# Residual rows and V leave PSUM by half rows; the layer-norm statistics and the row score read SBUF; shorter rstd; a new recorded order

## The chip, the cores and the metric

One core of a Trainium2 chip runs the kernel. The metric is the device time of one execution in microseconds (us), as the median of several runs. Comparisons are between kernels that ran in turn on the same chip, and only runs in the fast state are compared: ratios and intervals use these alone, while a median that is quoted is over all runs of its kernel, slow ones too. Engines are named as in the profile: PE is TensorE, DVE is VectorE, ACT is ScalarE, POOL is GpSimd.

## The reference, cut to what matters

The program is one transformer block over 2048 rows of 576 columns. Attention works on four segments of 512 rows with 32 heads of 18 columns and carries a memory from segment to segment. Then one single row, the one with the highest score, goes through an MLP.

```python
def A(x):                        # attention, S=2048, D=576, H=32, Dh=18, 4 segments of 512
    q, k, v = heads(x @ wq), heads(x @ wk), heads(x @ wv)
    phi = lambda t: where(t > 0, t + 1.0, exp(t))          # the feature map
    for s in range(4):
        p   = softmax(qs @ ks.T * Dh**-0.5 + mask)         # the 160 exponentials of the profile
        o   = (1 - g) * (p @ vs) + g * (phi(qs) @ M) / (phi(qs) @ z + 1e-6)
        M, z = M + phi(ks).T @ vs, z + sum(phi(ks))
    return o @ wo
def B(x):                        # MLP (F=4608) for the row with the highest score
    r = x @ w_r;  i = argmax(r)
    x[i] += sigmoid(r[i]) * ((silu(x[i] @ w_gate) * (x[i] @ w_up)) @ w_down)
    return x
x = x + ga * A(layernorm(x) * (1 + ca) + sa)
x = x + gb * B(layernorm(x) * (1 + cb) + sb)
```

## The kernel before

The kernel registers some thousand small operations, each with one or more engines that may do it, and then issues them in a recorded order. `ORDER` holds, for each place, the number of an operation and the engine chosen for it. It also holds dummy matmuls, which keep TensorE from falling idle.

```python
def recorded(self):
    ...
    for x in struct.unpack("<%dH" % (len(raw) // 2), raw):
        o = self.ops[x // 4]
        o.eng, _, o.emit = o.alts[x % 4]          # operation x//4, by its engine choice x%4
        seq.append(o)
```

The layer norms turn mean and variance into `rstd`, and then normalise a tile of 128 rows by 576 columns on whichever engine the order names.

```python
def rstd_op(mv, rst, i0, n, slot, R, W, eps=True):
    nm_ = nmr[:, slot, 0:n]
    def f():
        if eps:
            nc.gpsimd.tensor_tensor(out=mv[:, i0:i0+n, 1], in0=mv[:, i0:i0+n, 1], in1=epsF[:, 0:n], op=ALU.add)
        nc.gpsimd.tensor_tensor(out=rst[:, i0:i0+n], in0=mv[:, i0:i0+n, 1], in1=mhalf[:, 0:n], op=ALU.pow)
        nc.gpsimd.tensor_tensor(out=nm_, in0=mv[:, i0:i0+n, 0], in1=rst[:, i0:i0+n], op=ALU.mult)
        nc.gpsimd.tensor_scalar(nm_, nm_, -1.0, None, op0=ALU.mult)          # nmr = -mean * rstd
    ...
def norm_alts(dst, src, sc_, mn_, bi_, engs=("POOL", "DVE", "ACT")):
    a = {"POOL": ("POOL", 0.83, lambda: nc.gpsimd.tensor_scalar(dst, src, sc_, bi_, op0=ALU.mult, op1=ALU.add)),
         "DVE": ("DVE", 0.43, lambda: nc.vector.tensor_scalar(dst, src, mn_, sc_, op0=ALU.subtract, op1=ALU.mult)),
         "ACT": ("ACT", ac(576, "S", 1), lambda: nc.scalar.activation(dst, src, ACT.Identity, bias=bi_, scale=sc_))}
```

The feature map is built as min(max(t + 1, 1), exp(t)) in two VectorE operations. V and the output projection collect two halves of 288 columns in two PSUM banks, and the pair is copied out by one operation. The statistics and the score of the residual rows read the same two banks.

```python
# feature map, both on VectorE
nc.vector.tensor_scalar(PH, QT[0:r2, m0:m0 + np_, :], 1.0, 1.0, op0=ALU.add, op1=ALU.max)
nc.vector.tensor_tensor(out=PH, in0=PH, in1=EQK[0:r2, ei, 0:np_, :], op=ALU.min)
...
# residual rows of tile i (output projection plus the input, in PSUM)
g2 = P.psum("M", 2)
...
xp = lambda g2=g2: pair(g2)[:, :, 0:288]
op(alts(("ACT", ..., copy(xo, xp())), ("DVE", ..., tensor_copy(xo, xp()))), ...)       # one copy of 576 columns
ln_stats(lambda g2=g2: (bank(g2, 0)[:, 0:288], bank(g2, 1)[:, 0:288]), mv2[:, i, :], ...)
nc.vector.scalar_tensor_tensor(out=JK..., in0=xp(), scalar=mv2[:, i, 0:1], in1=W1B...,  # the score: x from PSUM
                               op0=ALU.subtract, op1=ALU.mult, accum_out=ra[:, i:i + 1])
rstd_op(mv2, rstd2, i, 1, sl, ...)
nc.gpsimd.tensor_tensor(out=rr[:, i:i+1], in0=ra[:, i:i+1], in1=rstd2[:, i:i+1], op=ALU.mult)
# finish_tile: UB = norm(x1), then three elementwise steps ("WB"), each on VectorE or GpSimd
tt(w_, u_, G1b, ALU.mult, ...); tt(w_, w_, C2b, ALU.add, ...); tt(w_, w_, xo, ALU.add, ...)
```

The softmax here doesn't subtract the row's maximum and nothing guards it: scores larger than these inputs give would overflow.

Of the kernel before, what the change touches and what calls it, by code (L numbers as in the profile page):

```python
# [35 lines left out]
    "Kml+7JOBs)bN~PWGyntu)Btz@>;OmrPynm|002w?3;>7$fB~2Qd;#PDU;vx|i~%?Rpa2j6fB<{|hyaiQumQ9Ix&hb$qyQ)Yr~niIpaIAM`~ZXjlmTo2=mFUP"  # L36
    "m;tZ=Q~+E6qyeA?yaB}lSO7!;!U4<yqz0S;cmeDIv;ffogaF(D)d4^NtOl?K<QM1{>=*DCWCDx;v<9dK@d4ohEC9R)AOP3`^Z_IS6au&g<pBf&C<6Ea7y<|a"
    "zy`Pg@Brul^Z+aZ3<A6WzyL4;r~w=T`~k!OoC4eeXaXSu-~#0WYyuDh^a4Zx00KM#(Ev08WB{N8%?6|cpaOsbtN|PVZ~~+P#Rg0Q7y$SJr~)_w$p%mYbONXY"
    "JOV)ikOQm(<Ob0O=mwYr_y(*3lmo~B%mCZ~=mOvX@CJkeR08w{L;_d>?FNVf00SHYTmp;&)CT<q*aqMRAOi#gBm)QoxB{F5FaT@=_zT?z1Ps6f{0sa73<I<R"
    "a08G6zyibryaIFs01OZVcmu=&$OB9RC<Dj>umjBkPy=8BTmw`Cv;zzbd;$akxC2N6U;}6X%mWAvxCgugkN{)@Sp$>;X#;oyoCnYXJOh9Ogaf<>Km&*ai~}?S"  # L40
    "zz0MF#Rtd-5DW+bNCOxH6bu*)APfuvBn;3400fu<Farbx)dQdh90Aw^2n09-BmfWu6a*Lq90a5X3<MAX_yFAl<O5g-s0ZK!Fb4n!@B{b*^aK0@TnFd_DGclb"
    "7zbbnGzT09AOvIwI0xJZJO?NQAP3+FBnRvQ91J7`umaQqKm>3EH~~cj<Oc)?bOh)JECVbAcmyB;2nP%Y6a#1nC<lB47y&Q@Kn#=sJPb?>SOriFL<|53WC1t?"
    "Tm=vZEDSIVGz3%(1PDnCU<7~%2nc8dWCTD3><2sqI1GdbfCw}U3<&rKR1r)E@B&y7cn63FfCLl)j0c1Sga}9lKnJV`L<NWhOa)vKEC+}PNCa#FbO($GO$1N{"
    "U<ix^pagsbYy@BdWD%qUWC(B!s06G8YzJrvZ3rj`ECEmlSPXmzR0Z@0R0LcMkOY_nv<FlNU<{N5)CY77Y!NI7cnq8bWDL*;Py{dtumpSzkO%MtGzhf>SOhc;"
    "P!U`N*bHD1Xc0IK+zj{x&;$?&^aS7x)CBYlJPr5^Yz1%y{0!IxKn-98*arX&NC@Q&`~=_xxCBrEXay7pcm*H`=mc;P<OF;XWCbJvyaaRwX#s!@PzXc^00sO9"
    "I0&!@R0voB2n7TMzyw$bgbmyTTnJPFfD!Bj%m>5-$OOy;bP+@dc@Zc9a0pBY5Cwb%6a^Rs90iCCbO;m(NCzAUh!G40cnCBBs1b|}@CV=)uneRTd<cXQAO)ZZ"
    "krAvBv<zqrxC|%-B?T}6j1jyHqzI4*s0geGm=P@nkPRdVZ~@2-lo6Z}%ndLF&<)51pb<0$m<W^zoCr7tzz94ANCAip)eXo9PzsC;JP2qCa0gThkPKJ~#0U@#"
# [12 lines left out]
    "@eAAwY!7q~IS+sfJP$k)m<vD;MGp`Y6cgAI7!$Y~yc>BB<O_fgC=aX>EDtabSQ2~>hz~3iFcWMLg%4Q^G!rxr%nOYVkPnp)Gz-8R#2XwFm=7QmoDaww%p1@f"  # L60
    ")En3v+#BE<<Qt3=pbw-EBoO!!Boq7+loP!WC=e(UkQ0~_a1eA5I1?-o025pbcn~lUJQG9{KobNLG!Wz#NE0{^2oro0uo4In%o2bTd=P{ah!cPigb+j!%oaTm"
    "Y!gfnuoiR^ND#;pkPws*OcQVuQ4_cpR1=60q!Z{H>>KbK^c(maOckgTSrd2@P!%i`R1h!}R22jfJO&IA{2Krq1RMw)WEC_N5D~l+z!10)oD+}>#1mW)pcZHq"
    "Y!$>1P!PZqm=K^4SQS_hp%e5ATouR=+!Lh>U=ZXJU=?H#I27O$%n;BJ+z`zZtQOD{$P?5P*%Q?e6cOMM7!hC-TodFFtP`*kv=d|#9TXrGj1Z^`=o7RSxDy-^"
    "*bpQXXcG(^5F8X77#tiNARG-8C=o0Xs1_*{L=+ShArb8m5ERH2sSxxN>=W@5_!FEEKoG4E85C#`un<TT@DL;%C>$&tFdQ@-Y!omNJQO4md=)_y{1fyL02ELZ"
    "OcVqZR1^plSQJDHfE6?mbQGx+v=DF<tQ4>mI1z9abQL%pJRCqAL>%Q5>=bwvq!7RsgcV2}OdL=gR2-NTh!u<#wG`+SycT#AJQ4U1{1E6CK@k8E%@xoUL=n^#"
    "ND&wo@f4sG6c>;cloebQoD{?spcSMQ*cD(D+!dr0WE7|s;1$#q>=u|6ycFCN>=kGfxD@CR<rNebfE0Wbz!a<%gcR@<*c9{?_!U?jTpVB=WE^N5Ar&YU{S}B5"
    "92blfAQzAnloT8m;1u{2Bp37){S*-uBo$y57!@cNEfq`=AQqez$Q1Y%#1zaF1Qh@k2o=y26crs6EEhBt=oJhXFc$z83>736WEQX$XcjaVFcmlzC>A^wKou+&"
    "L={LCcouCIa29+PbQXaYgcdj!JQk1^lotFJv=ulP02jFxKo&$6Y#eYLbR2jbd>nurgdB(*j2u80F&0S{m=>HCkQ|g8m>irOpd6$es2r>uupG1;xE#D3z#POJ"
    "L>EXG$Q;ZZ&>Ykp*c{v(;2h)}=p5`E@Er6U_#FHk038G!P#07eh!$EG2ptR^a2N0vycbLt1r~T0JQuwc^cFN02^PQ=To;TMP!?4d#1#w{5Epb8d>4clfEP>_"
    "2p0qwh!>0(kQbB}z!w-7#1{}2$QNN3WEW@`Y!_J;To%k1&=;5&pckYUoENAUuotWsv=_J+*ca3n+!x>%")  # L70
BANKS = (
    "00IF30S5vB0|o{F00#vE2Lb~nB@;IR6D1Q095(?a0RjL33LG3R3LG2?B>@Kq1_~ts69E$eB@-nD0s;XpHzgba0XHQ90|W#I1_lBF1px#T1rq=_1px*I00#vI"
    "2L=TL0wn=AB@;I{0TTfeH#ZXn1q2fTHxoA#0TUA?1qA^CH#ZXjH#a3WB>)5lB>@T?69F7I903Oa2LU%X69)tZ1_1yi10@1C022TQ1_K8L1p)&E2L%H+0RaIn"
    "903zI0US3RHwFU%0XHQ96E`;{B>?~i2LTfSB{wA{0TTfR2Ld+}6D0v9B@-n#0|EmI3KIbU2LS>%03`td03`(h0tEyG1O);F1popC024P80VM$eHvu;U1p_w|"
    "6E`;{0RjROB@;IR69fkb6D1`#903Ie1`{^{69oYQ6B8u_0uwhk69NY%0XHQB12;D}0R$xm0RsUCB?ABk0s;aD1TFvy1P2EL0|Ns900000000000000000000"
# [81 lines left out]
def mmc(n):  # L157
    return max(n / 2400 + 0.0025, 0.025)
# [11 lines left out]
def kernel(  # L170
# [1160 lines left out]
```

## Time and profile before

| | before |
|---|---|
| time, median of the first three runs | 261.76 us (261.16 to 262.21) |
| span of the profiled run, mean granted TensorE clock | 258.5 us, 0.972 |
| first, last of the 160 exponentials start | 25.8, 227.1 us |
| search for the highest score, MLP, down-projection start | 236.5, 242.5, 251.2 us |

The page's first part gives each engine's busy time, share of the span and number of instructions.

```profile
PE 230.6 (89%) x3447; PEld 142.9 (55%) x3466; DVE 212.6 (82%) x477; ACT 196.9 (76%) x236; POOL 171.5 (66%) x283
```

No engine is alone the limit. GpSimd has the lowest share of the four, 66%. The second part of the page cuts the span into 40 slices and gives the busy tenths of GpSimd in each.

```profile
POOL 6804723854939955596966879739679997818720
```

In the groups of instructions, kept apart by shape, the columns are line, engine, operation, output<-input names and shapes, count, then busy us and mean ns of one, then the idle us just before them and what ended it.

```profile
L748 ACT ACTIVATE arena<-PS 128x1024 bf16<-128x1024 f32 x160 | 152.7, 1028 | 16.8 <-PE PS L730 11.5 <-PE PS L739 2.2 <-POOL mv L541 1.8
...
L884 POOL TENSOR_TENSOR arena<-arena 128x576 bf16<-128x576 bf16 x21 | 27.6, 1320 | 6.0 <-DVE arena L883 5.6
...
L548 POOL TENSOR_SCALAR arena<-arena,rstd,nmr 128x576 bf16<-128x576 bf16 x15 | 13.8, 920 | 0.6
...
L937 DVE SCALAR_TENSOR_TENSOR arena<-PS,mv,arena 128x576 bf16<-128x576 f32 x16 | 13.0, 812 | 0.3
```

L748 are the exponentials: ScalarE idles 16.8 us before them, 11.5 of it for the score matmuls of L730. L548 is GpSimd's normalisation, 0.92 us each. L937 is the row score. The source view of two of these lines gives the least, median and greatest duration in ns.

```profile
L548 POOL TENSOR_SCALAR arena<-arena,rstd,nmr x15: 823/827/1833, 7.6 to 224.5; 128x576 bf16<-128x576 bf16 x15
```

```profile
L937 DVE SCALAR_TENSOR_TENSOR arena<-PS,mv,arena x16: 805/810/819, 102.2 to 233.6; 128x576 bf16<-128x576 f32 x16
```

The score never varies by more than 14 ns. The tail is a chain of single steps. The chain of waits lists start us, us, and what; these are three of its pieces.

```profile
235.20 1.41 DVE arena L549
...
246.08 1.51 DVE arena L883
...
247.68 0.46 DVE arena L883
```

L549 is a normalisation and L883 an elementwise step. The same L883 takes 1.51 us and then 0.46. Last, the table of stretches gives, for 252 to 254 us, the busy time of PE, PEld, DVE, ACT and POOL with counts, then the granted clock, the DMA share and GB/s; the timeline gives start and duration of the down-projection.

```profile
252.00:254.00 2.00, 2.00 (x76) 2.00 (x68) 0.01 (x1) 0.00 (x0) 0.00 (x0) 0.50 0.03 8
```

```profile
251.17 3.78 PE L1279 MATMUL PS<-arena 128*1 128x144 bf16 x144 [0.28 <-DVE arena L1243]
```

The down-projection runs at half clock (0.50) and takes 3.78 us.

### The profile page before, as it was taken

The numbers are of one execution on the slowest core, as the hardware profiler recorded it, in microseconds if no ns is written. First come the engines' busy times: TensorE is split into PE (matmuls) and PEld (weight loads), VectorE is DVE, ScalarE is ACT, GpSimd is POOL, SyncE is SP. The second block draws the span as 40 slices with busy tenths as digits, with TensorE's granted clock in tenths as the row PEclk, the third lists the DMA queues.
The fourth block names the chain that finished last, engine by engine and source line by source line (L and its number), as shares of the span: only waits on it lengthen the run. The fifth ranks groups of instructions, "written<-read, shape, count | busy, mean of one in ns | idle before, by whom it ended". The sixth has DMA issues, their size and how long they took to land. (4 is left out here: it accounts for less than half of the span.)

```text
span 258.5 us, 8600 instructions
## 1 busy us (share of the span) xinstructions
PE 230.6 (89%) x3447; PEld 142.9 (55%) x3466; DVE 212.6 (82%) x477; ACT 196.9 (76%) x236; POOL 171.5 (66%) x283
## 2 busy tenths in 40 slices
PE   7699899989999999999989999799878998887974
PEld 3364465445446566656555655466556766655544
DVE  4847977768999999999989879686879999889470
ACT  3452788888988999999889989599979799942030
POOL 6804723854939955596966879739679997818720
PEclk9979999999999999999999999799999999999787
DMA  5959963555746142474325289554788869998650
GB/s 158 324 161 285 319 184 122 163 165 173 199 115 180 55 116 94 129 230 147 118 71 186 79 251 268 187 170 160 217 268 278 263 218 281 229 326 324 207 191 3
DMA packets 34207, 49.20 MB, mean 190 GB/s; under 512 B 4011, under 2 KB 28210, under 8 KB 34166
## 3 DMA queue, kind: packets, MB, share of 16 engines
q1 hardware_dynamic: 34166, 48.64, 60.8%
q8 instruction: 27, 0.44, 0.7%
q14 instruction: 14, 0.11, 0.1%
HBM read 36.75 MB, written 11.87 MB: 188 GB/s over the span
## 5 line engine op out<-in xcount | busy, mean ns | idle before, releaser
L748 ACT ACTIVATE arena<-PS 128x1024 bf16<-128x1024 f32 x160 | 152.7, 1028 | 16.8 <-PE PS L730 11.5
L759 POOL TENSOR_SCALAR_AFFINE_SELECT arena<-arena 128x1024 bf16<-128x1024 bf16 (+1 forms) x65 | 64.9, 1007 | 37.1 <-ACT arena L748 31.7
L618 PE MATMUL PS<-arena 128*128 128x512 bf16 (+1 forms) x176 | 49.9, 385 | 2.7 <-DVE arena L622 1.0
L730 PE MATMUL PS<-arena 18*128 18x128 bf16 (+2 forms) x736 | 35.3, 259 | 4.7 <-DMA arena<-q_d 1.6
L884 POOL TENSOR_TENSOR arena<-arena 128x576 bf16<-128x576 bf16 x21 | 27.6, 1320 | 6.0 <-DVE arena L883 5.6
L730 PEld LDWEIGHTS <-arena 18*128 18x128 bf16 x736 | 16.1, 92 | 24.6 <-issue 21.4
L684 PE MATMUL PS<-arena 128*128 128x288 bf16 x160 | 26.2, 286 | 0.6 <-ACT arena L748 0.3
L774 PE MATMUL PS<-arena 128*32 128x128 bf16 (+2 forms) x736 | 24.3, 264 | 2.4 <-ACT arena L748 1.1
L618 PEld LDWEIGHTS <-arena 128*128 128x128 bf16 (+1 forms) x195 | 17.2, 102 | 16.6 <-issue 5.4
L920 PE MATMUL PS<-arena 128*128 128x288 bf16 x160 | 25.1, 286 | 1.0 <-ACT arena L748 0.6
L622 DVE CAST arena<-PS 128x512 bf16<-128x512 f32 (+1 forms) x29 | 19.3, 679 | 3.8 <-PE PS L618 1.6
L782 DVE CAST arena<-PS 128x512 bf16<-128x512 f32 (+1 forms) x27 | 17.7, 660 | 4.5 <-PE PS L774 4.3
L774 PEld LDWEIGHTS <-arena 128*32 128x32 bf16 x736 | 14.5, 97 | 11.4 <-issue 3.3
L1293 PE MATMUL PS<-arena 128*128 128x256 bf16 x135 | 19.8, 283 | 0.0
L684 PEld LDWEIGHTS <-arena 128*128 128x128 bf16 x160 | 14.1, 98 | 7.3 <-issue 2.0
L920 PEld LDWEIGHTS <-arena 128*128 128x128 bf16 x160 | 14.0, 97 | 7.0 <-issue 2.5
L541 POOL TENSOR_TENSOR mv<-mv,epsF 128x1 f32<-128x1 f32 (+2 forms) x21 | 4.1, 197 | 20.7 <-DVE mv L533 10.7
L883 DVE TENSOR_TENSOR arena<-arena 128x576 bf16<-128x576 bf16 x27 | 17.1, 645 | 0.2
L668 ACT ACTIVATE arena<-arena 128x1024 bf16<-128x1024 bf16 (+1 forms) x18 | 16.5, 927 | 0.0
L674 DVE TENSOR_TENSOR arena<-arena 126x1024 bf16<-126x1024 bf16 (+1 forms) x18 | 14.7, 819 | 0.5 <-ACT arena L668 0.4
L1293 PEld LDWEIGHTS <-arena 128*128 128x128 bf16 x135 | 12.3, 100 | 5.1 <-issue 3.3
L542 POOL TENSOR_TENSOR rstd<-mv,mhalf 128x1 f32<-128x1 f32 (+2 forms) x21 | 13.8, 657 | 1.6
(206 smaller groups left out, 413.0 us busy)
## 6 DMA issues: line engine op xcount, KB each, us to landing
arena<-in_B_w_down_dram SPq DMA_DIRECT2D x9, 576.0 KB
arena<-in_B_w_up_dram SPq DMA_DIRECT2D x8, 576.0 KB
arena<-in_B_w_gate_dram SPq DMA_DIRECT2D x8, 576.0 KB
arena<-in_A_x_dram SPq DMA_DIRECT2D x28, 144.0 KB
arena<-q_d SPq DMA_DIRECT2D x30, 128.0 KB
arena<-k_d SPq DMA_DIRECT2D x30, 128.0 KB
arena<-in_w_mod_dram SPq DMA_DIRECT2D x3, 1152.0 KB
x_d<-arena SPq DMA_DIRECT2D x16, 144.0 KB
```

Of the source, the lines that this page charges most:

```text
L618: nc.tensor.matmul(bank(g, 0)[0:r], lhsT=lhs(k), rhs=h1T[hb][:, k, :], start=(k == 0), stop=(k == KC - 1))
L622: op(alts(("DVE", dv(512, "P"), lambda g=g, dst=dst, r=r: nc.vector.tensor_copy(dst, bank(g, 0)[0:r])), ("ACT", ac(512), lambda g=g, dst=d ...
L684: nc.tensor.matmul(bank(g, hf)[:, 0:288], lhsT=h1T[hb][:, k, 128 * b:128 * b + 128], rhs=WP["v"][:, k, 288 * hf:288 * hf + 288], start=(k ...
L730: nc.tensor.matmul(bank(gs_[x // 2], x % 2)[:, off:off + b - a], lhsT=KS[32 * x:32 * x + DH, c, 128 * j:128 * j + 128], rhs=QS[32 * x:32 * ...
L748: op(one("ACT", 1.035, lambda g=gs_[x], pt=pt: nc.scalar.activation(pt, pair(g), ACT.Exp, scale=SCALE)), R=[("lt", n)], W=[("PT", pp, x)], ...
L759: om = op(alts(("POOL", 0.68 if pat[0][1] == 4 else 1.12, lambda v4=v4, pat=pat: nc.gpsimd.affine_select(out=v4, in_=v4, pattern=pat, comp ...
L774: nc.tensor.matmul(bank(gp, 0)[32 * x:32 * x + 32, o0 + a - qa:o0 + b - qa], lhsT=va[:, j, 4 * c + x, :], rhs=PT[:, pp, x, off:off + b - a ...
L782: ("DVE", dv(w, "P"), lambda gp=gp, ai=ai, gi=gi: nc.vector.tensor_copy(ASB[ai][:, gi, 0:w], bank(gp, 0)[:, 0:w]))),
L883: op(alts(("DVE", dv(576, acc=2), lambda: nc.vector.tensor_tensor(out=out_, in0=a_, in1=b_, op=o_)), ("POOL", 1.3, lambda: nc.gpsimd.tenso ...
L884: ("POOL", 1.3, lambda: nc.gpsimd.tensor_tensor(out=out_, in0=a_, in1=b_, op=o_))), R=R, W=W, lock=True)
L920: nc.tensor.matmul(bank(g2, hf)[:, 0:288], lhsT=ot[:, k, :], rhs=wop[:, k, 288 * hf:288 * hf + 288], start=(k == 0), stop=False)
L1293: op(one("PE", mmc(256), lambda gF=gF, src_=src_: nc.tensor.matmul(bank(gF, 0)[:, 0:256], lhsT=src_[:, 0:128], rhs=src_[:, 0:256], start=T ...
```

## The change

The intent: free PSUM banks earlier (halves, and statistics and score that no longer hold the banks), move work from VectorE to the less busy GpSimd, drop two of the four small operations of each `rstd`, compute the input statistics of segments 2 and 3 in the head, and record a new order for all of it. The diff, cut to its core:

```diff
@@ ORDER, BANKS: new strings, cut @@
@@ rstd_op, norm_alts @@
-        nm_ = nmr[:, slot, 0:n]
             nc.gpsimd.tensor_tensor(out=rst[:, i0:i0 + n], in0=mv[:, i0:i0 + n, 1], in1=mhalf[:, 0:n], op=ALU.pow)
-            nc.gpsimd.tensor_tensor(out=nm_, in0=mv[:, i0:i0 + n, 0], in1=rst[:, i0:i0 + n], op=ALU.mult)
-            nc.gpsimd.tensor_scalar(nm_, nm_, -1.0, None, op0=ALU.mult)
-    def norm_alts(dst, src, sc_, mn_, bi_, engs=("POOL", "DVE", "ACT")):
-        a = {"POOL": ("POOL", 0.83, lambda: nc.gpsimd.tensor_scalar(dst, src, sc_, bi_, op0=ALU.mult, op1=ALU.add)),
+    def norm_alts(dst, src, sc_, mn_, bi_, engs=("POOL", "DVE")):
+        a = {"POOL": ("POOL", 0.83, lambda: nc.gpsimd.tensor_scalar(dst, src, mn_, sc_, op0=ALU.subtract, op1=ALU.mult)),
@@ head: statistics of segments 2 and 3 (cut) @@
+    def ahead():
+        for s in (2, 3):
+            dma(xa, x_in[L * s:L * s + L, :]..., kb=590)
+            ... ln_stats(...); rstd_op(mv1, rstd1, TPS * s, 4, 0, ...)
@@ feature map @@
-                op(one("DVE", ..., nc.vector.tensor_scalar(PH, QT[...], 1.0, 1.0, op0=ALU.add, op1=ALU.max)), ...)
+                ts_ = lambda e, ...: ENG[e].tensor_scalar(PH, QT[...], 1.0, 1.0, op0=ALU.add, op1=ALU.max)
+                op(alts(("DVE", dv(512 * np_, acc=4), ... ts_("DVE")), ("POOL", 0.13 + 0.62 * np_, ... ts_("POOL"))), ...)
@@ V: the same for the residual rows @@
-            g = P.psum("M", 2)
+            for hf in range(2):
+                g = P.psum("M", 1)
                 ... five matmuls of 288 columns, then one copy of 288 columns
@@ residual rows @@
-            ln_stats(lambda g2=g2: (bank(g2, 0)[:, 0:288], bank(g2, 1)[:, 0:288]), mv2[:, i, :], RP, ..., ps=[g2])
-            op(one("DVE", 0.95, ... scalar_tensor_tensor(out=JK..., in0=xp(), ...)), ..., ps=[g2])
+            ln_stats(lambda xo=xo: (xo[:, 0:288], xo[:, 288:576]), mv2[:, i, :], RX, ...)
+            op(one("DVE", 0.82, ... scalar_tensor_tensor(out=JK, in0=xo, ...)), ...)
-            op(one("POOL", 0.15, ... rr[:, i] = ra[:, i] * rstd2[:, i]))            # for each tile
+            r0 = {7: 0, NT - 3: 8, NT - 2: NT - 2, NT - 1: NT - 1}.get(i)           # four times in all
```

Decoding the two orders shows what the new one does with the choices.

| | before | after |
|---|---|---|
| dummy matmuls | 135 | 106 |
| add/max of the feature map on GpSimd | 0 | 12 |
| elementwise steps at the end of a tile, GpSimd/VectorE | 21/27 | 30/18 |
| normalisations on GpSimd | 15 | 20 |
| copies of V, of residual rows | 16, 16 | 32 halves (25 on VectorE), 32 halves (22 on VectorE) |

## The prediction

> **What bounds the kernel now.** The engine summary shows TensorE busy 89%, VectorE 82%, ScalarE 76%, GpSimd 66%. No engine is alone the limit. In the table of stretches, 60–160 us has ScalarE 93%, VectorE 94% and TensorE 94% busy at full clock, but TensorE there includes idle-filling dummy matmuls (135 of 256 columns, 19.8 us of records). ScalarE's 160 exponentials (1.03 us each) set the floor; they idle 16.8 us in total, 11.5 of it waiting for score matmuls (groups view), which wait for PSUM banks and for VectorE's turn. The last 27 us are a serial tail (chain of waits from 234.4 us on): evacuation 0.67, a normalisation that took 1.41 beside a GpSimd operation (its own fastest: 0.33), top-1, the MLP, three elementwise steps (1.5+0.5 us) ahead of the gate, and a down-projection at granted clock 0.5–0.66.
>
> **What the change does.** I decoded both recorded orders.
> - Dummies fall from 135 to 106; sixteen of these are new in the MLP tail. Before the last tile's scores about 45 go: at 0.11–0.15 us, 5–6 us of TensorE holes closed, less 3 more masked score steps (about 0.5 us).
> - Two-bank residual groups, held through statistics, score product and copy (about 2.5 us after the last matmul at 230.7–235), become single banks freed by a half copy.
> - VectorE: 12 feature max operations (−6 us), 9 elementwise (−5.8) and 2 normalisations go to GpSimd; 6 h1T evacuations arrive (+3.2); copies in halves cost about 0.46 (from 0.55 for 384 and 0.73 for 576 columns), +4 us. Net about −8. ScalarE −3.
> - GpSimd: about −13 us (two operations of each rstd, 12 of 16 score products), but about +30 of moved work: net about +15.
> - Eight statistics (8.8 us VectorE) and 1.2 MB of loads move into the head, where VectorE is 60–85% busy but the DMA share is 1.03 at 20–30 us: I expect the first exponential 0–2 us later (25.8 before).
> - Tail: last copy and normalisation leave VectorE's path ahead of top-1 (−1 to −1.5 us), elementwise work moves ahead of the MLP's end (−0.5 to −1), dummies keep the clock up for the down-projection (−0.5 to −1.2; the Trainium skill, "TensorE: Matmul & The Clock Gate", What's actually happening: half rate after an idle window of about 3.4 us; the trace agrees, 0.50 at 252–254).
>
> **Brakes.** The score product now has two SBUF inputs. The Trainium skill, "SBUF — State Buffer", Who interferes with whom, says such a VectorE instruction and a GpSimd one that reads SBUF exclude each other. The trace agrees for other operations: the elementwise step takes 0.44 to 1.52 us, the normalisation 0.33 to 2.09. With 15 us more GpSimd work and 16 such products I expect these waits to eat about half of VectorE's −8. Estimate: body −2.5, head +0.5, tail −2.5 us.
>
> **Prediction: 257.2 us, 80% range 253.3 to 260.6.** Faster by over 2%: 0.39; within 2%: 0.58; slower: 0.03.
>
> **What would show each step right or wrong.** Dummies about 106. Residual and V copies about 0.46 us on VectorE and 0.42 on ScalarE. ScalarE's waits for score matmuls below 11.5 us. VectorE busy 203–212, GpSimd 182–190 us. Score product mean from 0.81 to 0.8–1.2 us, with a long maximum. Last exponential 2–3 us earlier than 228.1; from there to the end about 2.5 us less. Down-projection clock above 0.8.
>
> **What would make it wrong.** If exclusion between GpSimd and VectorE is mild, the closed holes count in full: 253–255. If the statistics in the head, queued ahead of the first score operands on VectorE, delay the first exponential by over 3 us, or masks now later behind GpSimd's new work stall the probability products, the time stays at 260–262.

## The result, and the profile after

The kernel after takes 294.04 us (median of four runs, 293.72 to 299.05, the last of them slow), beside 261.46 us for the kernel before (median of four). The ratio is 1.1248, with a 95% interval of 1.119 to 1.1306. Ratios here and below are from the fast runs of both kernels in the same rounds, so not quite the ratio of the medians quoted. The result is correct. The mean granted clock of the profiled runs fell too, from 0.972 to 0.924; what that costs by itself was not separated.

The page's first part and GpSimd's row of the second, after:

```profile
PE 237.7 (81%) x3501; PEld 142.2 (49%) x3501; DVE 218.5 (75%) x482; ACT 195.0 (67%) x240; POOL 236.9 (81%) x249
...
POOL 7453594999799999988899249999969999299971
```

GpSimd went from 171.5 to 236.9 us busy, 65 us more, with 34 fewer instructions. I had predicted 182 to 190. Its row is now nearly all 9. The fourth part of the page, the chain that ended last, by engine:

```profile
POOL 36%; PE 32%; DVE 15%; issue 9%; ACT 6%; DMA 1%; SPq 0%; POOLq 0%; ACTq 0%; DVEq 0%
```

GpSimd leads it with 36%. The groups that answer to those of before, with the two of the moved add/max (L685):

```profile
L763 ACT ACTIVATE arena<-PS 128x1024 bf16<-128x1024 f32 x160 | 152.5, 1031 | 36.6 <-PE PS L745 25.2 <-PE PS L754 10.1 <-PE PS L789 0.4
L547 POOL TENSOR_SCALAR arena<-arena,mv,rstd 128x576 bf16<-128x576 bf16 x20 | 49.1, 2458 | 0.8
...
L899 POOL TENSOR_TENSOR arena<-arena 128x576 bf16<-128x576 bf16 x30 | 39.1, 1309 | 3.1 <-DVE arena L898 2.2
...
L685 POOL TENSOR_SCALAR arena<-arena 126x1024 bf16<-126x1024 bf16 x7 | 25.4, 3634 | 0.0
...
L961 DVE SCALAR_TENSOR_TENSOR arena<-arena,mv 128x576 bf16<-128x576 bf16 x16 | 15.4, 960 | 0.1
...
L685 POOL TENSOR_SCALAR arena<-arena 72x512 bf16<-72x512 bf16 x5 | 10.1, 2024 | 0.0
```

```profile
L547 POOL TENSOR_SCALAR arena<-arena,mv,rstd x20: 2285/2320/3252, 13.1 to 272.7; 128x576 bf16<-128x576 bf16 x20
```

```profile
L961 DVE SCALAR_TENSOR_TENSOR arena<-arena,mv x16: 765/814/1556, 110.9 to 268.6; 128x576 bf16<-128x576 bf16 x16
```

Three things are to be seen. GpSimd's normalisation has the same engine, instruction name and shape as before, but takes 2.46 us instead of 0.92; even its fastest took 2.285, against 0.823. That speaks against waiting beside another engine and for an operation that is slower itself; micro, below, tests it. The twelve add/max cost 35.5 us in all; scaling 0.92 us for 576 columns, I had put them near 1.3 us each, some 15.5. And the exponentials now wait 35.3 us (25.2 + 10.1) for matmuls. The elementwise step of L899 costs 1.31 us as before, so GpSimd has not become slower in general.

The sum works out. Twenty normalisations at (2.46 − 0.92) are 30.8 us, the add/max 20.0 more than assumed, together 51 us. That fits the gap between the 236.9 us and the 182 to 190 predicted (47 to 55).

How a long GpSimd operation reaches the exponentials shows in the timeline between 66 and 78 us: start us, us, engine, line, what, and in brackets the idle time before and its releaser.

```profile
66.77 3.66 POOL L685 TENSOR_SCALAR arena<-arena 126x1024 bf16<-126x1024 bf16 x1
...
70.47 6.10 DVE L687 TENSOR_TENSOR arena<-arena 126x1024 bf16<-126x1024 bf16 x1 [2.50 <-POOL arena L685]
...
76.60 1.06 ACT L682 ACTIVATE arena<-arena 128x1024 bf16<-128x1024 bf16 x1 [6.81 <-DVE arena L687]
...
76.99 1.01 PE L632 MATMUL PS<-arena 128*128 128x512 bf16 x2 [7.02 <-DVE arena L705]
```

VectorE waits 2.50 us for GpSimd's add/max; its minimum, L687, then takes 6.10 us beside five GpSimd operations in a row; ScalarE stands 6.81 us and TensorE 7.02. In ScalarE's own timeline no exponential runs between 69.8 and 78.6 us.

In one place the tail looks as was hoped.

```profile
286.00:288.00 2.00, 2.00 (x105) 1.77 (x106) 1.03 (x4) 0.00 (x0) 0.00 (x0) 1.00 0.21 74
```

```profile
286.56 2.42 PE L1306 MATMUL PS<-arena 128*1 128x144 bf16 x144
```

The clock is 1.00 here and the down-projection takes 2.42 us instead of 3.78. That the new dummies did this is not shown: before_norm, an experiment told below, has the tail of the kernel before with none of them, and ran the same matmuls as fast.

```profile
258.75 2.42 PE L1279 MATMUL PS<-arena 128*1 128x144 bf16 x144 [0.28 <-DVE arena L1243]
```

The milestones, read from the timelines, tell where the time went:

| start us | before | after | both | modelled | modelled_score1 |
|---|---|---|---|---|---|
| first exponential | 25.8 | 27.5 | 26.9 | 25.5 | 26.4 |
| 41st | 87.0 | 99.7 | 89.4 | 89.2 | 91.7 |
| 121st | 182.4 | 206.1 | 180.3 | 182.1 | 180.2 |
| last exponential | 227.1 | 260.8 | 231.7 | 231.6 | 228.2 |
| search for the highest score | 236.5 | 273.2 | 242.5 | 242.2 | 237.8 |
| down-projection | 251.2 | 286.6 | 254.8 | 255.4 | 251.0 |
| end of span | 258.5 | 292.4 | 260.6 | 261.2 | 256.8 |

The last exponential starts 33.7 us later, and the whole span is 33.9 longer. The loss lies in the body; the tail is a wash. (The last three columns are experiments told below.)

### The profile page after: what moved, and what is told of

The parts are those of the page before. It is cut to its first block, busy times and chain, and to the rows that moved or that the text cites. A ratio compares the mean times of both kernels' runs of the same rounds, so it can differ in the third digit from the quotient of the medians.

```text
span 292.4 us, 8676 instructions
## 1 busy us (share of the span) xinstructions
PE 237.7 (81%) x3501; PEld 142.2 (49%) x3501; DVE 218.5 (75%) x482; ACT 195.0 (67%) x240; POOL 236.9 (81%) x249
## 4 chain that ended last, share of the span: by engine, by line
POOL 36%; PE 32%; DVE 15%; issue 9%; ACT 6%; DMA 1%; SPq 0%; POOLq 0%; ACTq 0%; DVEq 0%
POOL arena L547 10%; POOL arena L774 9%; PE PS L632 8%; POOL arena L685 7%; ACT arena L763 5%; POOL arena L899 4%; PE PS L935 4%; PE PS L745 3%; DVE arena L916 3%; POOL rstd L543 3%; PE PS L789 2%; PE PS L1320 2%; PE PS L1228 2%; PE PS L652 2%; PE PS L615 1%
## 5 line engine op out<-in xcount | busy, mean ns | idle before, releaser
L763 ACT ACTIVATE arena<-PS 128x1024 bf16<-128x1024 f32 x160 | 152.5, 1031 | 36.6 <-PE PS L745 25.2
L774 POOL TENSOR_SCALAR_AFFINE_SELECT arena<-arena 128x1024 bf16<-128x1024 bf16 (+1 forms) x62 | 61.7, 1009 | 20.5 <-ACT arena L763 20.3
L632 PE MATMUL PS<-arena 128*128 128x512 bf16 (+1 forms) x195 | 57.0, 402 | 8.9 <-DVE arena L705 7.0
L547 POOL TENSOR_SCALAR arena<-arena,mv,rstd 128x576 bf16<-128x576 bf16 x20 | 49.1, 2458 | 0.8
L899 POOL TENSOR_TENSOR arena<-arena 128x576 bf16<-128x576 bf16 x30 | 39.1, 1309 | 3.1 <-DVE arena L898 2.2
L685 POOL TENSOR_SCALAR arena<-arena 126x1024 bf16<-126x1024 bf16 (+1 forms) x12 | 35.5, 2963 | 0.0
L935 PE MATMUL PS<-arena 128*128 128x288 bf16 x160 | 29.3, 303 | 3.8 <-DVE arena L819 2.2
L632 PEld LDWEIGHTS <-arena 128*128 128x128 bf16 (+1 forms) x195 | 18.4, 105 | 26.3 <-issue 16.8
L699 PE MATMUL PS<-arena 128*128 128x288 bf16 x160 | 27.5, 289 | 0.2 <-ACT arena L763 0.2
L745 PEld LDWEIGHTS <-arena 18*128 18x128 bf16 x736 | 15.2, 95 | 25.5 <-issue 22.8
L687 DVE TENSOR_TENSOR arena<-arena 126x1024 bf16<-126x1024 bf16 (+1 forms) x18 | 19.4, 1089 | 4.8 <-POOL arena L685 4.4
L935 PEld LDWEIGHTS <-arena 128*128 128x128 bf16 x160 | 14.3, 103 | 11.1 <-issue 3.9
L699 PEld LDWEIGHTS <-arena 128*128 128x128 bf16 x160 | 14.1, 98 | 7.7 <-issue 1.7
L1320 PE MATMUL PS<-arena 128*128 128x256 bf16 x106 | 17.6, 297 | 0.0
L924 PE MATMUL PS<-arena 128*128 128x128 bf16 x80 | 8.4, 243 | 9.8 <-DVE arena L916 9.5
```

The source lines that it names most:

```text
L632: nc.tensor.matmul(bank(g, 0)[0:r], lhsT=lhs(k), rhs=h1T[hb][:, k, :], start=(k == 0), stop=(k == KC - 1))
L685: ts_ = lambda e, PH=PH, QT=QT, r2=r2, m0=m0, np_=np_: ENG[e].tensor_scalar(PH, QT[0:r2, m0:m0 + np_, :], 1.0, 1.0, op0=ALU.add, op1=ALU.max)
L687: mn_ = lambda e, PH=PH, ei=ei, r2=r2, np_=np_: ENG[e].tensor_tensor(out=PH, in0=PH, in1=EQK[0:r2, ei, 0:np_, :], op=ALU.min)
L699: nc.tensor.matmul(bank(g, 0)[:, 0:288], lhsT=h1T[hb][:, k, 128 * b:128 * b + 128], rhs=WP["v"][:, k, 288 * hf:288 * hf + 288], start=(k = ...
L745: nc.tensor.matmul(bank(gs_[x // 2], x % 2)[:, off:off + b - a], lhsT=KS[32 * x:32 * x + DH, c, 128 * j:128 * j + 128], rhs=QS[32 * x:32 * ...
L763: op(one("ACT", 1.035, lambda g=gs_[x], pt=pt: nc.scalar.activation(pt, pair(g), ACT.Exp, scale=SCALE)), R=[("lt", n)], W=[("PT", pp, x)], ...
```

## The experiments

Three theories were put to the test. Theory A: the cost comes from the form of GpSimd's operations, because (x − mean)·rstd and max(t + 1, 1) take far longer there than x·rstd + nmr. Theory B: the operations are not slower themselves, but GpSimd and VectorE now exclude each other from SBUF more often. Theory C: the new order, the half copies and the statistics in the head are to blame. B has a basis: the Trainium skill, "SBUF — State Buffer", Who interferes with whom, says that a VectorE instruction with two SBUF inputs contends with a GpSimd instruction that reads SBUF, and that one with at most one SBUF input, outside certain modes, does not. Sixteen kernels ran. Their line numbers are their own.

### micro: the disputed operations alone

Not the kernel, but a list of GpSimd operations on tiles of the same shapes, three of each form, meant to run with VectorE idle. Its output is wrong.

```diff
+for _ in R: g.tensor_scalar(D, A, p0, p1, op0=ALU.mult, op1=ALU.add)        # L27
+for _ in R: g.tensor_scalar(D, A, p0, p1, op0=ALU.subtract, op1=ALU.mult)   # L28
+for _ in R: g.tensor_scalar(D, A, p0, p1, op0=ALU.add, op1=ALU.mult)        # L30
+for _ in R: g.tensor_scalar(d[:], a[:], 1.0, 1.0, op0=ALU.add, op1=ALU.max) # L34, 1024 columns
+for _ in R: g.tensor_scalar(d[:], a[:], 1.5, 2.5, op0=ALU.mult, op1=ALU.add)# L35, 1024 columns
+... eleven more forms; L31 and L32 are mult/add and subtract/mult with constants
```

> A kernel of its own, wrong result on purpose: GpSimd runs single tensor-scalar forms three times each on 128x576 bf16 with VectorE idle, then four times eight GpSimd operations in a row with one VectorE operation waiting beside them. Theory A (form: the GpSimd operation itself is slow with operations other than multiply-then-add): (mult, add) about 0.83 us, (subtract, mult) about 2.3 us, (add, max) about 2.0 us at 576 and 3.6 us at 1024 columns, all alone on the chip. Theory B (port exclusion: the form costs nothing, VectorE's use of the shared port stretched it in the kernel): all forms about 0.83 us here. Second half, starvation: if back-to-back GpSimd operations keep VectorE out, the two-input VectorE operation takes some 8 us or waits until the row ends instead of its 0.45 us; if not, at most about 1.7 us. The statistics operation, which reads one tensor, stays near 0.45 us.

Measured, in the timeline (start us, us for all of the count):

```profile
6.21 0.82 POOL L27 TENSOR_SCALAR d<-a,p 128x576 bf16<-128x576 bf16 x1
...
10.91 7.06 POOL L28 TENSOR_SCALAR d<-a,p 128x576 bf16<-128x576 bf16 x3
...
25.24 2.66 POOL L30 TENSOR_SCALAR d<-a,p 128x576 bf16<-128x576 bf16 x3
27.99 2.18 POOL L31 TENSOR_SCALAR d<-a 128x576 bf16<-128x576 bf16 x3
30.25 6.58 POOL L32 TENSOR_SCALAR d<-a 128x576 bf16<-128x576 bf16 x3
...
43.58 11.04 POOL L34 TENSOR_SCALAR d<-a 128x1024 bf16<-128x1024 bf16 x3
54.70 3.30 POOL L35 TENSOR_SCALAR d<-a 128x1024 bf16<-128x1024 bf16 x3
```

| pair of operations on GpSimd, bf16 | 576 columns | 1024 columns |
|---|---|---|
| mult, then add (per-row scalars; constants) | 0.82; 0.73 us | (constants) 1.10 us |
| add, then mult (per-row scalars) | 0.89 us | |
| subtract, then mult (per-row scalars; constants) | 2.35; 2.19 us | |
| mult, then subtract | 2.36 us | |
| add, then add | 2.35 us | |
| add, then max (constants) | 2.19 us | 3.68 us |
| max, then add (constants) | 2.19 us | |
| mult alone; subtract alone (per-row scalar) | 1.79; 1.79 us | |

With nothing on VectorE, the form alone makes the factor: 2.19 against 0.73 with constants. The figures are thirds of a row of three, but for one. Beside the three of L27 the scheduler had drawn forward the VectorE operations that were meant for the second half; these three took 1.12, 0.82 and 1.40 us, and the least is in the table. With that the second half, the test of starvation, failed, and starve (below) repeats it in a fixed order. Of the pairs tried, only mult/add and add/mult are fast. Between 576 and 1024 columns, add/max costs (3.68 − 2.19) / 448 = 3.3 ns a column, mult/add 0.83. A single operation is slower than the fast pair. So A's mechanism holds, and the 2.46 and 3.63 us of the kernel are these costs (2.35 and 3.68) with hardly anything added.

### norm_form, phi_dve, both: each form undone alone, then both

The order is kept. In norm_form the normalisation is x·rstd + nmr again, with the two small operations it needs; in phi_dve the twelve add/max go back to VectorE at the same places; both does both.

```diff
 # norm_form
+            nc.gpsimd.tensor_tensor(out=nm_, in0=mv[:, i0:i0 + n, 0], in1=rst[:, i0:i0 + n], op=ALU.mult)
+            nc.gpsimd.tensor_scalar(nm_, nm_, -1.0, None, op0=ALU.mult)
-        a = {"POOL": (..., nc.gpsimd.tensor_scalar(dst, src, mn_, sc_, op0=ALU.subtract, op1=ALU.mult)),
+        a = {"POOL": (..., nc.gpsimd.tensor_scalar(dst, src, sc_, bi_, op0=ALU.mult, op1=ALU.add)),
 # phi_dve
-                op(alts(("DVE", ..., ts_("DVE")), ("POOL", 0.13 + 0.62 * np_, ..., ts_("POOL"))),
+                op(alts(("DVE", ..., ts_("DVE")), ("DVE", ..., ts_("DVE"))),
```

> The kernel after, with only the GpSimd normalisation back to multiply-then-add (20 operations), and with the two small GpSimd operations that make its -mean*rstd column again. Theory A: the 20 fall from 2.46 to 0.83-0.92 us each, GpSimd busy falls by about 32 us less 10 for the small operations, and the time falls by about half of the loss, to 274-282 us. Theory B: they stay near 2.4 us. Theory C (order, half-row copies and statistics in the head cost the time): under 4 us gained, 290 or more.

> The kernel after, with only the 12 add-then-max operations back on VectorE, at the same place in the order. Theory A: GpSimd busy falls by about 35 us, VectorE rises by about 6, the long waits of two-input VectorE operations (5.4 and 6.1 us) go; 274-283 us. Theory C: 290 or more. If VectorE is what limits, the 6 us show up as time.

> The kernel after, with both: normalisation on GpSimd as multiply-then-add, add-then-max on VectorE. Everything else of the change stands: new order, half-row copies, statistics and score from SBUF, head statistics, batched score products. Theory A: the whole loss goes, 255-264 us, GpSimd busy about 180 us. Theory C: 275 or more stays. Between these two, the rest is shared.

| | median us | before, same rounds | ratio (95%) | GpSimd busy | exponentials' wait for score matmuls |
|---|---|---|---|---|---|
| norm_form | 281.81 | 260.18 | 1.087 (1.071 to 1.1029) | 218.6 | 27.9 |
| phi_dve | 279.9 | 260.18 | 1.0803 (1.0655 to 1.0951) | 205.1 | 23.6 |
| both | 262.55 | 260.18 | 1.0096 (0.9858 to 1.0334) | 190.1 | 15.9 |

(The last column sums the two lines that name score matmuls; it was 13.7 before and 35.3 after.) From the groups of both:

```profile
L551 POOL TENSOR_SCALAR arena<-arena,rstd,nm 128x576 bf16<-128x576 bf16 x20 | 20.4, 1021 | 1.1 <-POOL nm L547 0.3
```

Alone, the two forms give back 12.2 and 14.1 us; together 31.5 of the 32.6 that the change cost. The two parts are not additive (26.3). Perhaps GpSimd stays near the limit in those stretches while one form remains; that was not tested. With both gone, the order, the half copies and the statistics in the head are all still there, and the ratio's interval includes 1, though it is wide. C is therefore not the main cause. At the 2% mark the record's verdict is unclear for each of the three, with only three rounds each; the intervals of the first two lie well above 1.

### modelled: cheap forms at no cost in operations

norm_form and both add small operations, and both loads VectorE. To get what I had in mind when I predicted, this kernel keeps every operation of the kernel after on its engine and only replaces the slow pairs by fast ones of equal shape. Its arithmetic is wrong (mean added instead of subtracted, mult/add instead of add/max), though the deviation stays within the tolerance of the comparison.

```diff
-        a = {"POOL": (..., nc.gpsimd.tensor_scalar(dst, src, mn_, sc_, op0=ALU.subtract, op1=ALU.mult)),
+        a = {"POOL": (..., nc.gpsimd.tensor_scalar(dst, src, mn_, sc_, op0=ALU.add, op1=ALU.mult)),
-                    PH, QT[...], 1.0, 1.0, op0=ALU.add, op1=ALU.max)
+                    PH, QT[...], 1.0, 1.0, op0=ALU.add if e == "DVE" else ALU.mult, op1=ALU.max if e == "DVE" else ALU.add)
```

> The kernel after, wrong on purpose: on GpSimd the normalisation is add-then-multiply (sign of the mean wrong) and the 12 max operations are multiply-then-add, both forms that took 0.89 us per 576 and 1.10 per 1024 columns alone. No operation more or fewer than in the change. This is the change at the durations that the prediction put in. If the remainder of the prediction was sound: 254-260 us, GpSimd about 180 us. If the order, half copies and head statistics earn nothing: 260-265, as both forms mended did (262.6). If 270 or more, a cause besides the forms is there.

Measured: 263.1 us (262.39 to 269.45, two of its runs slow) beside 260.01; ratio 1.0108 (1.006 to 1.0156). GpSimd is busy 185.8 us, inside the 182 to 190 of the prediction. VectorE is busy 217.4 us, not 203 to 212. The page's first part, then from the groups:

```profile
PE 228.4 (87%) x3482; PEld 139.0 (53%) x3501; DVE 217.4 (83%) x482; ACT 194.5 (74%) x240; POOL 185.8 (71%) x249
...
L961 DVE SCALAR_TENSOR_TENSOR arena<-arena,mv 128x576 bf16<-128x576 bf16 x16 | 18.4, 1153 | 0.1
L547 POOL TENSOR_SCALAR arena<-arena,mv,rstd 128x576 bf16<-128x576 bf16 x20 | 18.2, 910 | 0.8
...
L685 POOL TENSOR_SCALAR arena<-arena 126x1024 bf16<-126x1024 bf16 x7 | 7.3, 1047 | 1.3 <-PE PS L863 1.3
```

So the counts of moved work in my prediction were right, and the price of an operation was wrong. But even at the price I assumed, the kernel is 1.1% slower than before, not 1.7% faster. A second error was left to find. The score takes 1.153 us on average instead of 0.81. Ten of the sixteen still take about 0.8; six take 1.01 to 3.42.

### mended: a correct version with fast forms

(x + (−mean))·rstd uses the fast pair add/mult; it needs one small operation for −mean. The add/max go back to VectorE.

```diff
+        def gp():
+            nc.gpsimd.tensor_scalar(bi_, mn_, -1.0, None, op0=ALU.mult)
+            nc.gpsimd.tensor_scalar(dst, src, bi_, sc_, op0=ALU.add, op1=ALU.mult)
```

> The kernel after, correct: normalisation on GpSimd as (x + (-mean)) * rstd, with one small operation of 0.25 us for -mean, add-then-max on VectorE. 258-263 us: as the run with both restored, less one small operation for each of 21 rstd; GpSimd near 185 us. Beats the kernel before only if it comes under 258.

Measured: 266.87 us (262.13 to 269.25) beside 260.01; ratio of fast runs 1.0137 (1.0065 to 1.0209). Four of its six runs were slow, the fast ones took 264.95 and 262.13. By the interval a correct mend lies near modelled, and it does not beat the kernel before.

### before_norm and before_addmult: the form alone, in the old kernel

before_norm changes one line of the kernel before, the normalisation's form on GpSimd (15 times). before_addmult uses the fast pair add/mult there, and drops the `nmr` operations where possible.

```diff
 # before_norm
-        a = {"POOL": (..., nc.gpsimd.tensor_scalar(dst, src, sc_, bi_, op0=ALU.mult, op1=ALU.add)),
+        a = {"POOL": (..., nc.gpsimd.tensor_scalar(dst, src, mn_, sc_, op0=ALU.subtract, op1=ALU.mult)),
 # before_addmult
+            nc.gpsimd.tensor_scalar(bi_, mn_, -1.0, None, op0=ALU.mult)
+            nc.gpsimd.tensor_scalar(dst, src, bi_, sc_, op0=ALU.add, op1=ALU.mult)
```

> The kernel before, with nothing changed but the form of the 15 normalisations on GpSimd: subtract-then-multiply. Theory A: each goes from 0.92 to 2.3-2.5 us, GpSimd busy up by about 22 us (171 to 193), the kernel slower by 5-14 us, 266-275, though GpSimd stays under 76% busy. If GpSimd's slack hides it (it waits 37 us for exponentials): 260-263.

> The kernel before, with the normalisation on GpSimd as add-then-multiply of -mean: one small operation fewer and the other no longer behind rstd. GpSimd busy down by about 3 us (171 to 168). Time the same within 1%, 258-262; a gain of 1 us at most, because these operations seldom lie on the chain.

before_norm: 268.33 us beside 260.01; ratio 1.0336 (1.0286 to 1.0387). Its group:

```profile
L548 POOL TENSOR_SCALAR arena<-arena,mv,rstd 128x576 bf16<-128x576 bf16 x15 | 34.9, 2329 | 0.2 <-PE PS L618 0.2
```

One changed line, with no new order and no half copies, costs 3.4%. It added 21 us of GpSimd time (34.9 − 13.8), and some 8 of them came through to the end, although GpSimd was busy only 72% of the span. before_addmult: 262.62 (257.98 to 265.57), ratio 0.9996 (0.9915 to 1.0076), from only two fast runs of six. With the other fast form, and fewer small operations, no difference is seen.

### norm_dve: both forms on VectorE at the same places

```diff
-        a = {"POOL": ("POOL", 0.83, lambda: nc.gpsimd.tensor_scalar(...)),
+        a = {"POOL": ("DVE", 0.43, lambda: nc.vector.tensor_scalar(dst, src, mn_, sc_, op0=ALU.subtract, op1=ALU.mult)),
```

(and the add/max as in phi_dve)

> Correct: the kernel after, both slow forms on VectorE, at the same place in the order; no extra operation anywhere. GpSimd busy near 155 us (237 less 49 and 35), VectorE up by 20 x 0.43 + 6 us and by fewer waits for the port. If GpSimd's slack shortens the exclusions more than VectorE's added 15 us cost: 256-260, faster than before. If VectorE limits: 261-266.

Measured: 275.59 us beside 261.08; ratio 1.059 (1.0505 to 1.0674). VectorE is busy 225.3 us, GpSimd 158.8, and GpSimd waits 57.8 us for exponentials. That is above both branches of the expectation. A likely reading, not isolated, is that work taken off GpSimd in this order has no free place on VectorE either.

### starve and starve2: how VectorE fares beside GpSimd

Rows of GpSimd operations of 1.3 us each, and one VectorE operation beside each row; all but the statistics also run alone. Their outputs are wrong, which doesn't matter for the times.

```diff
+g.tensor_tensor(out=h[:], in0=A, in1=b[:], op=ALU.mult)
+for _ in range(5): g.tensor_tensor(out=d[:, 0:576], in0=A, in1=b[:], op=ALU.mult)
+nc.vector.tensor_tensor(out=r[:], in0=h[:], in1=b[:], op=ALU.add)   # or tensor_scalar, scalar_tensor_tensor, bn_stats
```

> A kernel of its own, wrong result on purpose, its order fixed by hand: seven GpSimd operations of about 1.3 us in a row, and one VectorE operation that may start after the second of them. Starvation (rows of GpSimd operations keep a VectorE operation out that reads two tensors from SBUF): the two-input operation, 0.45 us alone, ends only when the row ends, 5-7 us, as the 6.1 and 5.4 us records of the kernel after. Plain exclusion, one turn each: at most 0.45 + 1.3 us, and the GpSimd row 0.45 us longer. The statistics operation (one tensor): 0.45 us in both.

In the timeline, the first row of five, and then three VectorE operations beside such rows:

```profile
5.12 6.76 POOL L35 TENSOR_TENSOR d<-a,b 128x576 bf16<-128x576 bf16 x5
5.20 1.51 DVE L37 TENSOR_TENSOR r<-h,b 128x576 bf16<-128x576 bf16 x1 [1.53 <-POOL h L30]
...
26.41 1.81 DVE L41 SCALAR_TENSOR_TENSOR r<-h,p,b 128x576 bf16<-128x576 bf16 x1 [9.19 <-POOL h L30]
...
46.70 0.46 DVE L43 BATCH_NORM_STATS2 st<-h 128x6 f32<-128x288 bf16 x1 [8.08 <-POOL h L30]
```

Alone, the same two-input addition takes 0.46 us and the score's kind 0.82. Beside the row they take 1.51 and 1.81: about 1 us longer, less than one GpSimd operation, then they get through. The statistics, with one SBUF input, are not touched (0.46 us; 0.445 on average on SBUF rows in the kernel before). For these three the page's rule holds. But a subtract/mult on VectorE with one SBUF tensor, in the same run, took 1.36 us beside its row and 0.43 alone. One input alone does not keep an operation free; whether this is the page's exception for certain modes, no run here tests. (The normalisation that the prediction names beside the two-input rule, 0.33 to 2.09 us, is such an operation too, and so no case of that rule.) In these rows B is a mild brake, one turn for each such operation. It costs GpSimd little: the row of five took 7.06 us beside the score's kind and 6.67 beside the statistics, 0.4 us apart, where 51 us were to be explained.

But one turn does not explain the 6.10 us of L687 in the kernel after, which outlasted five GpSimd operations, and that record is not alone. VectorE records over 3 us stand in four of the profiles. Besides the 6.10 they are, in order, of the kernel after, norm_form, modelled (two, the second a score) and modelled_score1 (below):

```profile
156.66 5.39 DVE L916 TENSOR_TENSOR arena<-arena 128x576 bf16<-128x576 bf16 x1
...
66.04 6.09 DVE L691 TENSOR_TENSOR arena<-arena 126x1024 bf16<-126x1024 bf16 x1 [2.22 <-POOL arena L689]
...
61.40 3.92 DVE L687 TENSOR_TENSOR arena<-arena 126x1024 bf16<-126x1024 bf16 x1
...
161.42 3.42 DVE L961 SCALAR_TENSOR_TENSOR arena<-arena,mv 128x576 bf16<-128x576 bf16 x1
...
62.67 4.79 DVE L687 TENSOR_TENSOR arena<-arena 126x1024 bf16<-126x1024 bf16 x1
```

All four kernels have the feature map's first step on GpSimd; no kernel that has it on VectorE shows such a record. So in the kernels B is not always mild. starve2 rebuilt the row around the 6.10 us beside a minimum of 128x1024, and beside smaller operations:

```diff
+g.tensor_scalar(h[:], a[:], 1.0, 1.0, op0=ALU.add, op1=ALU.max)
+aff(); tt(); aff(); tt(); aff()          # select, product, select, product, select on GpSimd
+g.tensor_scalar(D, A, p0, p1, op0=ALU.subtract, op1=ALU.mult)
+nc.vector.tensor_tensor(out=r[:], in0=h[:], in1=c4[:], op=ALU.min)
+... three variants of it
```

> A kernel of its own, wrong result on purpose. It lays out the row of GpSimd operations that stood beside the 6.1 us VectorE operation of the kernel after: add-then-max, then mask selections (one SBUF input) and two-input products in turn, then subtract-then-multiply; a two-input VectorE operation may start after the first. If the alternation lets GpSimd keep the port: 5-7 us for that operation, in the variants with selections and products in turn, and about 1.4-2 us in the variant of products and multiply-then-adds or in none. If it is one turn here too: at most 2 us in all, and the 6.1 us stay unexplained.

Measured: the minimum took 1.50 us in both of its rows, the smaller operation 1.27 and 1.51. The long one was not reproduced. Why these records are so long, and what they cost in the end, stays open.

### modelled_score1: the score's second SBUF input taken away

modelled, but the score is computed by a VectorE operation with a single SBUF tensor (the weights are left out, so the scores are wrong).

```diff
-            op(one("DVE", 0.82, ... nc.vector.scalar_tensor_tensor(
-                out=JK, in0=xo, scalar=mv2[:, i, 0:1], in1=W1B, op0=ALU.subtract, op1=ALU.mult, accum_out=ra[:, i:i + 1])),
+            op(one("DVE", 0.82, ... nc.vector.tensor_scalar(
+                JK, xo, mv2[:, i, 0:1], 0.0, op0=ALU.subtract, op1=ALU.add, accum_out=ra[:, i:i + 1])),
```

> The run with cheap forms (263.1 us), and besides, wrong on purpose, the score product made by an operation that reads one tensor from SBUF instead of two (16 of them; they took 1.15 us each there, 0.77 at the fastest, 0.81 from PSUM in the kernel before). If exclusion by GpSimd of the score product is what eats the gain: it falls to about 0.77-0.8 us each, and the time to 258-260 us. If the gain is missing for other reasons: within 1 us of 263.

Measured: 258.45 us (256.92 to 259.91) beside 260.17; ratio 0.9944 (0.9893 to 0.9996). The group:

```profile
L961 DVE TENSOR_SCALAR_CACHE_REDUCE arena<-arena,mv 128x576 bf16<-128x576 bf16 x16 | 12.8, 798 | 0.1
```

The score is back at 0.80 us, VectorE at 210.7 us busy, and the exponentials' wait for the score matmuls (the larger of the two lines) is 9.8 us, against 15.1 in modelled. Between the fast runs of modelled and of this kernel lie 4.3 us (means of 262.84 and 258.54; two chips, with nearly equal times of the kernel before) for 5.6 us of score time (18.4 − 12.8). So the score's second SBUF input, where the kernel before had read its rows from PSUM, is a part of the second error. It is not all of it. By the milestones, the body from the first to the last exponential takes 201.3 us before, 206.1 in modelled and 201.8 here, and the prediction had wanted it 2.5 us shorter than before. Some 3 us are not accounted for, and what this kernel gains on the kernel before it gains in the tail (28.6 us after the last exponential's start, 31.4 before).

### before_sbuf, before_sbuf1, half_score: the score's source in other settings

before_sbuf lets statistics and score of the kernel before read SBUF after the copy, with the order otherwise kept; unlike in the change, the PSUM banks stay held until both are done. before_sbuf1 also gives the score one input. half_score is mended with the score taken from PSUM by halves, beside the half copies.

```diff
 # before_sbuf
-            ln_stats(lambda g2=g2: (bank(g2, 0)[:, 0:288], bank(g2, 1)[:, 0:288]), mv2[:, i, :], RP, ...)
+            ln_stats(lambda xo=xo: (xo[:, 0:288], xo[:, 288:576]), mv2[:, i, :], [("x1", xi)], ...)
-                out=JK..., in0=xp(), scalar=mv2[:, i, 0:1], in1=W1B...
+                out=JK, in0=xo, scalar=mv2[:, i, 0:1], in1=W1B,
 # half_score
+                    nc.vector.scalar_tensor_tensor(out=JK[:, c_], in0=bank(g, 0)[:, 0:288], scalar=1.0, in1=W1B[:, c_],
+                                                   op0=ALU.mult, op1=ALU.mult, accum_out=(ra, rb)[hf][:, i:i + 1])
```

> The kernel before with one part of the change alone: statistics and score read the bf16 copy in SBUF instead of PSUM, after the copy; the order is kept but for what must wait for the copy. If the part hurts by exclusion and by waiting for the copy: score 0.81 to 1.0-1.2 us each, 262-266 us. If it helps (bank freed by the copy): 257-260.

> The kernel before with statistics and score from SBUF (273.6 us), and besides, wrong on purpose, the score product by an operation that reads one tensor. If the exclusion of the score product cost the 13 us: 260-264. If waiting for the copy (with the order of before, made for statistics straight from PSUM) cost it: 270-274.

> Correct: the kernel after with both forms mended (add-then-multiply of -mean, add-then-max on VectorE), and the score product taken from PSUM in halves beside each half copy, without the mean (the mean times the sum of the weights is taken off later, in a few small operations). The products then read one tensor from SBUF. Against the mended kernel (266.9, fast runs 1.4% over before): if exclusion of the score product is the rest of the loss, 257-261 us, 0 to 1% faster than before; if not, 262-266. Its risk is that two products of 0.46 us cost more VectorE time than one of 0.81.

| | median us | before, same rounds | ratio (95%) |
|---|---|---|---|
| before_sbuf | 273.63 | 260.17 | 1.0427 (1.0352 to 1.0502) |
| before_sbuf1 | 269.17 | 260.68 | 1.0393 (1.0314 to 1.0472) |
| half_score | 273.87 | 260.68 | 1.0565 (1.0491 to 1.064) |

In the old order most of the loss remains when the score reads one input, so most of it has another cause. That statistics and score now wait for the copy is likely, but was not isolated. The part of the second input can't be told there, as the intervals overlap. before_sbuf and half_score came out above both branches of their expectations. half_score failed as a mend: the 32 halves cost 0.448 us each, more than sixteen whole scores, and VectorE waited 6.5 us for ScalarE's copies. Neither says anything against the reading of modelled_score1, and neither confirms it.

### before_tail: only the tail's pieces

The kernel before, with dummies ahead of the transposes for the up-projection and of the down-projection, the normalisation of tile 14 on ScalarE, and the first output step of the last tile moved ahead.

```diff
+            if u:
+                keep(13)
...
     def down():
+        keep(3)
```

> The kernel before, with the parts of the change that seemed to help after the last exponential, and no other: dummies ahead of the last transposes and of the down-projection, which ran its 144 matmuls in 3.8 us at half clock before and in 2.4 after; the normalisation of tile 14 (1.41 us on VectorE beside GpSimd, in the way of the top-1 search) on ScalarE, which idles; the first output step of tile 15 ahead of the copies for the last row, so that its other two steps do not block VectorE ahead of the gate. 1.4 + 0.8 + 1.0: 257-259 us, and faster than both kernels by 1 to 1.5% of before. If the clock does not follow: 259-260.

Measured: 260.31 us beside 260.17; ratio 1.002 (0.9969 to 1.0071). The 257 to 259 us that were hoped for did not come. The down-projection took 2.4 us instead of 3.8, as in the kernel after. The dummies held the transposes back by about 1 us, and the MLP's matmuls took 6.04 us instead of 4.73, since they stood in a stretch at half clock. But before_norm and before_sbuf1, without these dummies, ran the down-projection in 2.42 us too, and in before_norm the same MLP matmuls took 5.77. Where the half clock falls thus differs between profiles whose tails hold the same matmuls, and one profile does not tell what the dummies did.

## Why the prediction was wrong, and where it was right

**The step that failed** is, in its own words, "about +30 of moved work: net about +15" for GpSimd. The operations were counted rightly; modelled, with the same counts, has GpSimd at 185.8 us, inside the 182 to 190 predicted. The price was wrong. I had taken the 0.92 us of the normalisation before as the price of any one-tensor operation of that size on GpSimd. But the diff changes the pair of operations, and on GpSimd the pair sets the price: subtract/mult 2.35 us instead of 0.82, add/max 3.68 us instead of 1.10 for mult/add. The diff itself showed the changed pair, with the cost note 0.83 left standing beside it. On VectorE the form subtract/mult had long been in use at 0.43, so it looked harmless. This term was worth about 51 us of GpSimd time, and undoing both forms brought back 31.5 of 32.6 us.

**"ScalarE's waits for score matmuls below 11.5 us"**: 25.2 and 10.1 us in the kernel after, wrong mostly for the same reason: 11.8 and 4.1 with both forms undone, 11.5 and 2.2 before. But modelled has 15.1 and 2.5, so the line would have failed at the assumed prices too.

**"I expect these waits to eat about half of VectorE's −8"** was wrong too. In modelled, VectorE is at 217.4 us, 4.8 above the kernel before, so all of the −8 and more were eaten, if it was counted rightly. So "body −2.5" would have failed even with the prices that I assumed: modelled's last exponential starts 4.5 us later than before, not 2 to 3 earlier. Taking the score's second SBUF input away brought VectorE to 210.7 us and the time to 258.45, both inside the predicted ranges. That is luck and no confirmation: it removes a brake that I had counted in, and in its profile the body is still 0.5 us longer than before, not 2.5 shorter. The direction of this brake was right, and the score's own mean time was in the range that I gave; what it costs on the path, 4.3 us between modelled and modelled_score1, was mis-sized, and the rest stays open.

**"Tail −2.5"**: net +0.2 us from the last exponential to the end (31.6 us after, 31.4 before, by the milestones). The down-projection at clock 1.00 gave 1.4 us, a little more than the 0.5 to 1.2 predicted; as before_norm has the same without the dummies, this may be luck. But the search for the highest score comes 12.4 us after the last exponential instead of 9.4, with a GpSimd normalisation of 2.3 us in that stretch. In both, with fast forms, it is 10.8. At the prices I had assumed the tail does get shorter: 29.6 us in modelled, 28.9 in both and 28.6 in modelled_score1, 1.8 to 2.8 less than before. So this term seems to have failed through the slow forms, while the body's would have failed without them.

**Right**: 106 dummies; half copies 0.44 us on VectorE and 0.40 to 0.41 on ScalarE (predicted 0.46 and 0.42); the score 0.96 us on average with a maximum of 1.56 (predicted 0.8 to 1.2 "with a long maximum"); the first exponential 1.7 us later (predicted 0 to 2). No run took the statistics out of the head, so what they cost there is not measured.

**What stays open**: the VectorE records of 3.4 to 6.1 us, some 3 us of the body in modelled_score1, and whether the dummies set the clock of the down-projection. And no correct version of the change beat the kernel before: the one that does, by 0.6% with an interval that just excludes 1, computes a wrong score.

## What to carry to other kernels

In these runs an operation's duration belongs to its engine, its shape and its pair of operations together; when a diff swaps the arithmetic of a tensor_scalar on GpSimd, or moves one there, measure that pair on that engine before costing it, and never scale from another pair or from VectorE. An engine at 66% busy has no free third: 21 us more on GpSimd in the old kernel cost 8 us at the end. Before a PSUM operand is exchanged for an SBUF one on VectorE, count the SBUF inputs that the instruction has then; in these runs a second one made it wait beside GpSimd, mostly by one turn, a few times by several.

## What the Trainium skill lacked or had wrong

- "GPSIMD Engine Reference", 3.1 Elementwise — side-by-side cycle accounting, costs an element by the number of operations and inputs (about 2.6 cycles for two inputs, about 1.8 at best in a tight loop, 1.03 for bodies of up to two operations), and does not say that the time depends on which operations are paired. The runs show 0.82 us for mult/add, 0.89 for add/mult, and 2.35 for subtract/mult, mult/subtract and add/add at 128x576 in bf16; 0.83 ns a column for mult/add against 3.3 for add/max. A single mult (1.79 us) is slower than mult/add.
- "SBUF — State Buffer", Who interferes with whom, agrees for single operations (an addition 0.46 us alone, 1.51 beside GpSimd; statistics 0.46 beside it). It does not say how long a VectorE operation can be kept waiting by several GpSimd operations in a row: the test rows show one turn, the kernel after 6.10 us beside five operations and 5.39 us in a second place, which no run here explained.
